# GateLoop attention with a SwiGLU feed-forward on one core: norm roots spread through a line in device memory, ten pairs by 15 products, group 0 in chunks, and a schedule with other costs and dates

## The chip, the cores and the metric

The kernel runs on one core of one Trainium2 chip. The metric is the device time of one execution in microseconds (us), with all data in device memory at the start and the output there at the end. Smaller is better. Five engines work side by side: TensorE (PE, the matrix products; PEld is its weight load), VectorE (DVE), ScalarE (ACT), GpSimd (POOL) and SyncE (SP, which here only issues transfers). Each runs its own instructions strictly in the order in which they were written, so one instruction that waits holds up all behind it on that engine.

## The reference

Two blocks follow one another. The first is a gated linear attention with complex decay (batch 4, 8 heads, 768 steps, head size 48); the second is an RMS norm with a SwiGLU feed-forward (3072 tokens, width 384, hidden width 1536).

```python
mag = np.sqrt(a_re * a_re + a_im * a_im)
scale = np.minimum(mag, 0.999) / (mag + 1e-06)
a_re_n, a_im_n = (a_re * scale, a_im * scale)
for t in range(S):
    new_re = ar * S_re - ai * S_im
    new_im = ar * S_im + ai * S_re
    S_re, S_im = (new_re + kv, new_im)          # kv: outer product of k and v at t
    y[:, :, t] = np.einsum('bhd,bhde->bhe', q[:, :, t], S_re)
...
xn = x / np.sqrt(np.mean(x * x, axis=-1, keepdims=True) + 1e-06) * rms_g
g = xn @ w_gate
return (g * (1.0 / (1.0 + np.exp(-g))) * (xn @ w_val)) @ w_out
```

## The kernel before

**Chunks, units and groups.** The 3072 tokens are 24 chunks (n = 0 to 23) of 128. The decays of the first two chunks are worked out one by one (units 0 and 1), then two chunks at a time (units 2 to 12). The feed-forward takes two chunks together, a group: group g holds chunks 2g and 2g + 1.

**A unit (`gates`).** ACT takes squares, roots, arctangent and sines, and DVE takes running products and running sums over time. This gives the turned queries and keys. In a buffer called `rot` (and, for later chunks, in place in `kin`) they stand in the order of the input; six DMAs of SP per chunk put them into `kq`, where the heads lie as the products want them. For units 0 and 1 the decay at the end of the chunk is spread by DVE into `ot` and by a small PE product `bank<-ot,ot`; for later units by small DMAs (`decay<-ends`).

**A chunk (`attend`).** PE makes the scores (`bank<-kq`, 32 rows at a time); DVE masks them into `am` (`COPY_PREDICATED`); PE makes the output y from `am`, `ve` (the values), `kq` and `state`, and the new state (`bank<-ident,kq`, ACT copies to `kt`, then `bank<-vn,kt`). For the norm, ACT squares y into `sq`, PE adds over features (`bank<-ones,sq`), DVE scales into `ssv`, and POOL takes the inverse root `rs`, one number per token, in a column over 128 partitions. It is wanted as a row on all partitions. For chunks 0 to 3, 22 and 23 PE does that (`bank<-ident,rs`). For chunks 4 to 21 (`SENT`) POOL sends two DMAs: `rs` into a line within partition 0 of `sq`, and that line to all partitions of `row`. Then DVE multiplies y by it into `xT`, the normalized input of the feed-forward.

**The feed-forward.** Groups 0 to 2 (`PLAIN = 3`) go through `feed`: per block b of six, three 128x256 products for each of two halves of `w_gate` and as many for `w_val`, ACT's Silu into `sg`, DVE's product into `hT`. Groups 3 to 11 go through `joint`: the product of the two chunks with the weights is made from 15 products with sums of weights and sums of inputs in place of 18. `forms` makes those sums of weights once, 28 operations of DVE on 128x512, into room that single chunks used before: `gin[1]`, `rots[1]`, `kqs[1]`, `ams[1]`. From chunk `SOLO = 6` on, therefore, only one buffer each of `kq`, `am` and `rot` is in use. Per group, 12 DVE operations on 128x128 make the sums of inputs. Products per block are 15, each four 128x128 matmuls. From group 2 on the second half of the feed-forward (`down`) also saves products. A 128x512 product with zeros (`bank<-zeros`) opens a bank where a sum must be added to.

**Weights.** `narrow` brings the float64 weights in pieces: POOL issues the DMA, ACT converts the low word, and three operations of DVE put the number together (`TENSOR_SCALAR`, `SCALAR_TENSOR_TENSOR`, and a third that the profile calls `CUSTOM_DVE_ANT_0` and the order listing `ISA`). Six pieces are for `wg` and `wv` (128x1536 each), six for `wo` (128x768 each). A one-element copy on POOL (`junk`) waits for each piece's landing.

**What sets the order.** All operations are collected in a list with their engine, an estimated duration and what they depend on. `Flow.dates` gives each a due time, back from the feed-forward products; a table `flow.shift` then moves single stages by some us. `Flow.schedule` plays the program through: each engine that is free takes, of its operations that are ready by the estimate, the one with the earliest due time. The estimates of that play (how long a DMA takes to land, what a change of engine costs) thus decide the order in which the instructions are written, and the chip then runs them in that order whatever the true times are. Where PE has nothing to do in the first 62 us, warm matmuls (`bank<-rot`) are put in.

```python
    SYNC = 0.12
    LAND = 2.0
...
                    o["landed"] = now + o["slow"] + self.LAND + (1.5 if o["eng"] == "POOL" else 0.0)
...
    PLAIN = 3
    WIDE = 12
    SOLO = 6
...
            line = sq[0:1, 1]
            dma(line, rss[n % 2], "POOL", slow=SLOW)
            dma(wide, line.unsqueeze(1).to_broadcast([1, P, C]), "POOL", slow=SLOW)
```

Nearly all instructions carry the line of `Flow.issue` (L715) in the profile, so they are told apart by the names of what they write and read.

Of the kernel before, what the change touches and what calls it, by code (L numbers as in the profile page):

```python
# [8 lines left out]
FP32 = mybir.dt.float32  # L9
# [9 lines left out]
P = 128  # L19
# [481 lines left out]
class Flow:  # L501
# [6 lines left out]
    SYNC = 0.12  # L508
    LAND = 2.0
# [4 lines left out]
    TABLES = {"silu": ("S",), "sin": ("S", "T"), "arctan": ("T",), "rsqrt": ("A",)}  # L514

    def __init__(self, nc, rooms):
        self.nc = nc
        self.rooms = rooms
        self.ops = []
        self.seen = {}  # L520
        self.stage = None
        self.shift = {}
        self.warm = None
        self.fillers = []

# [36 lines left out]
    def add(self, eng, calls, dur, reads=(), writes=(), table=None, land=None, due=None, after=(), behind=(), late=None, mode=None, group=None):  # L562
        op = dict(i=len(self.ops), eng=eng, calls=calls, dur=dur, deps=set(), table=table, land=land,
# [31 lines left out]
    def schedule(self):  # L595
# [6 lines left out]
        mode = None  # L602
# [5 lines left out]
        lanes = {}  # L608
        sent = []
        recent = []  # L610
        now = 0.0
        order = 0

        def release(o, end, users=users):
            for u in users[o["i"]]:
                x = self.ops[u]
                lat = self.SYNC if x["eng"] != o["eng"] or o["land"] is not None else 0.0
                ready[u] = max(ready[u], end + lat)
# [3 lines left out]

        def flows(t):
            busy = [q for q in lanes.values() if q]
            whole = sum(q[0][1]["packet"] for q in busy)
            for q in busy:
                q[0][0] -= (t - now) * q[0][1]["packet"] / whole

        while True:
# [10 lines left out]
            busy = [q for q in lanes.values() if q]  # L640
            if busy:
                whole = sum(q[0][1]["packet"] for q in busy)
                q = min(busy, key=lambda q: q[0][0] / q[0][1]["packet"])
                t = now + max(0.0, q[0][0]) * whole / q[0][1]["packet"]
                if best is None or t <= best[0]:
                    flows(t)
                    now = max(now, t)
                    o = q.pop(0)[1]
                    o["landed"] = now + o["slow"] + self.LAND + (1.5 if o["eng"] == "POOL" else 0.0)
# [31 lines left out]
            if eng == "PE" and o["mode"] != mode:  # L681
                mode = o["mode"]
                dur += 0.06
            if eng == "PE" and self.warm and t < self.warm["until"] and all("end" in x for x in self.warm["after"]):
                since = max([free["PE"]] + [x["end"] + self.SYNC for x in self.warm["after"] if not recent])
# [12 lines left out]
            free[eng] = t + dur  # L698
            release(o, t + dur, self.next)
            if o["land"] is not None:  # L700
                flows(t)
                now = max(now, t)
                if eng != "POOL":
                    sent.append(o)
                lanes.setdefault(eng, []).append([o["load"] + 0.05, o])
# [12 lines left out]
def fast(tc, ctx, qT, kT, v, a_re, a_im, w_gate, w_val, w_out, rms_g, out, H, bad):  # L718
# [19 lines left out]
    PLAIN = 3  # L738
    WIDE = 12
    SOLO = 6  # L740
# [16 lines left out]

    outside = {x.tensor.name for x in (qT, kT, v, a_re, a_im, w_gate, w_val, w_out, rms_g, out)}
    keep = []
    banks = []  # L760
# [38 lines left out]
    def scan(o, d0, d1, init, op0, op1, **kw):  # L799
        return add("DVE", [(nc.vector.tensor_tensor_scan, (),  # L800
                            dict(out=o, data0=d0, data1=d1, initial=init, op0=op0, op1=op1))],
                   0.10 + 2.38e-3 * cols(o), aps(d0, d1, init), [o], **kw)
# [12 lines left out]
    def act(o, x, func, scale=None, bias=None, accum=None, **kw):  # L815
# [5 lines left out]
        if accum is not None:  # L821
            k["accum_out"] = accum
        dur = 0.17 + 0.86e-3 * cols(o) + 0.09 * len(aps(scale, bias)) + (0.19 if accum is not None else 0.0)
        return add("ACT", [(nc.scalar.activation, (), dict(out=o, in_=x, func=func, **k))], dur,
                   aps(x, scale, bias), aps(o, accum), table=TABLE.get(func), **kw)
# [11 lines left out]
    def dma(o, x, eng="SP", slow=0.0, **kw):  # L837
# [4 lines left out]
        load = n / row * (0.006 + 50.3e-6 * row) / 16  # L842
        op = add(eng, [(QUEUE[eng].dma_start, (), dict(out=o, in_=x))], 0.85 if eng == "POOL" else 0.62, [x], [o],
# [3 lines left out]
        op["packet"] = max(0.07, 0.006 + 50.3e-6 * row * (2 if eng == "POOL" and row == 2048 else 1))  # L847
# [126 lines left out]
    def fetch(i, piece, raw, eng):  # L974
# [13 lines left out]
        if eng == "POOL":  # L988
            landed[i] = add("POOL", [(nc.gpsimd.tensor_copy, (), dict(out=junk, in_=raw[0:1, 1:2]))], 0.8,
                            after=[sent])  # L990
# [5 lines left out]
    def narrow(i):  # L996
# [3 lines left out]
        if ap.dtype == FP32:  # L1000
            dma(to, ap.rearrange("(c p) f -> p c f", p=P)[:, c, f:f + n], "POOL")
            return
# [672 lines left out]
```

## Time and profile before

| | us |
|---|---|
| three runs, median | 700.45 |
| three runs, lowest to highest | 699.45 to 700.63 |
| the profiled execution, its own time | 701.28 |
| its span, first to last instruction | 699.5 |
| granted TensorE clock over it | 0.989 of full |

The profile gives, for each engine, its busy time, the same in 40 slices of the span, the chain of work that ended last, and groups of instructions. The trace behind it lists single instructions: start in us from the span's start, duration in us, engine, line, operation, what it writes and reads, its shape, how many were put together, and in square brackets the idle time of the engine before it and what ended that. A matrix product in float32 counts as two matmuls in the trace and as one in the program.

### The profile page before, as it was taken

Reading aid. Unit: us, or ns where it says so; the run is one execution under the profiler, and the core shown is the slowest. Engines: PE = TensorE matmul, PEld = TensorE weight load, DVE = VectorE, ACT = ScalarE, POOL = GpSimd, SP = SyncE. Lnnn points to the kernel's source line nnn. Section 1 sums busy time; section 2 is a strip of 40 time slices with the busy share of each in tenths; the row PEclk is TensorE's granted clock in tenths of the full one; section 3 lists DMA queues with packets and bytes.
Section 4 is the critical chain, followed back from the end, with each engine's and each line's share of the span. In section 5 each row is a group of like instructions: output and inputs, shape, how many; then the busy total and the mean of one; then the engine's idle time right before and its main releaser. Section 6 shows DMA issues by size and latency. Waiting matters only on the chain.

```text
span 699.5 us, 18714 instructions
## 1 busy us (share of the span) xinstructions
PE 657.1 (94%) x7792; PEld 607.5 (87%) x7792; DVE 559.4 (80%) x1017; ACT 477.9 (68%) x807; POOL 59.7 (9%) x108
## 2 busy tenths in 40 slices
PE   0698999999999999999999999999999998999995
PEld 0587867886889999998999999999999998999995
DVE  8989888869888788888788889888898896356462
ACT  8657777898654675574675684675674884688884
POOL 3122100011000001000101010001000010000000
PEclk9989999999999999999999999999999999999999
DMA  9995462535424243434504334424623543834422
GB/s 292 291 290 178 154 166 75 148 65 106 111 57 103 60 82 62 134 77 86 128 17 80 96 70 96 126 60 86 133 53 75 119 97 112 250 94 145 149 72 91
DMA packets 104012, 81.98 MB, mean 117 GB/s; under 512 B 41936, under 2 KB 94416, under 8 KB 103920
## 3 DMA queue, kind: packets, MB, share of 16 engines
q1 hardware_dynamic: 98560, 64.78, 34.6%
q0 software_dynamic: 4416, 15.35, 10.3%
q8 instruction: 62, 1.02, 0.6%
q10 hardware_dynamic: 944, 0.59, 0.3%
q14 instruction: 30, 0.25, 0.1%
HBM read 55.84 MB, written 4.72 MB: 87 GB/s over the span
## 4 chain that ended last, share of the span: by engine, by line
PE 79%; DVE 7%; ACT 6%; DMA 3%; SPq 2%; issue 2%; POOL 0%; DVEq 0%; ACTq 0%
PE bank L715 79%; SPq L715 2%; DMA kq<-kin 2%; ACT turns L715 2%; ACT L715 1%; DVE hT L715 1%; DVE rot L715 1%; ACT t L715 1%; DVE wv L715 1%; DVE turns L715 1%; DMA in<-in_a_im_dram 1%; DVE wg L715 1%; DMA in<-in_a_re_dram 1%; DVE t L715 1%; DVE in L715 0%
## 5 line engine op out<-in xcount | busy, mean ns | idle before, releaser
L715 PE MATMUL bank<-wo,hT 128*128 128x192 f32 (+1 forms) x696 | 143.7, 352 | 0.9 <-DVE hT L715 0.9
L715 PEld LDWEIGHTS bank<-wo,hT 128*128 128x128 f32 x696 | 115.5, 191 | 13.3 <-DVE hT L715 1.8
L715 PE MATMUL bank<-xT,wg 128*128 128x128 f32 (+1 forms) x504 | 98.2, 330 | 0.0
L715 PE MATMUL bank<-xT,wv 128*128 128x128 f32 (+1 forms) x504 | 94.3, 321 | 0.0
L715 PEld LDWEIGHTS bank<-xT,wg 128*128 128x128 f32 x504 | 80.2, 194 | 7.4 <-issue 0.4
L715 PEld LDWEIGHTS bank<-xT,wv 128*128 128x128 f32 x504 | 79.1, 192 | 5.9 <-ACT turns L715 0.2
L715 ACT ACT_TABLE_LOAD x51 | 65.4, 1283 | 7.3 <-DVE t L715 2.8
L715 ACT ACTIVATE hT<-bank 128x512 f32<-128x512 f32 x90 | 52.4, 594 | 25.9 <-PE bank L715 23.1
L715 POOL TENSOR_TENSOR rs<-ssv,mhalf 128x1 f32<-128x1 f32 x24 | 20.6, 858 | 479.0 <-DVE ssv L715 428.3
L715 ACT ACTIVATE sg<-bank 128x512 f32<-128x512 f32 (+1 forms) x72 | 38.9, 540 | 21.1 <-PE bank L715 17.9
L715 DVE TENSOR_TENSOR hT<-hT 128x768 f32<-128x768 f32 (+1 forms) x58 | 50.5, 871 | 1.1
L715 ACT ACTIVATE bank<-bank 128x512 f32<-128x512 f32 x54 | 31.5, 583 | 26.8 <-PE bank L715 18.9
L715 ACT ACTIVATE kt<-bank 128x384 f32<-128x384 f32 x40 | 19.5, 489 | 43.9 <-PE bank L715 34.8
L715 DVE COPY_PREDICATED am<-causal,bank 128x512 f32<-128x512 int32 x48 | 34.7, 731 | 16.0 <-PE bank L715 15.9
L715 PE MATMUL bank<-yg,wg 128*128 128x128 f32 x288 | 45.7, 281 | 0.0
L715 PE MATMUL bank<-sums,hT 128*128 128x192 f32 x240 | 44.7, 328 | 0.1
L715 PE MATMUL bank<-yg,wv 128*128 128x128 f32 x288 | 43.9, 275 | 0.0
L715 DVE TENSOR_TENSOR hT<-bank,hT 128x512 f32<-128x512 f32 x45 | 30.9, 688 | 14.8 <-ACT bank L715 7.8
L715 PEld LDWEIGHTS bank<-kq 96*32 96x32 f32 x1536 | 31.3, 112 | 12.6 <-issue 4.5
L715 PE MATMUL bank<-kq 96*32 96x128 f32 (+3 forms) x1536 | 37.0, 240 | 5.4 <-DMA kq<-kin 3.6
L715 ACT ACTIVATE turns<-in 128x768 f32<-128x768 f32 (+1 forms) x39 | 30.4, 791 | 13.8 <-DVE kin L715 12.7
L715 PEld LDWEIGHTS bank<-sums,hT 128*128 128x128 f32 x240 | 39.3, 190 | 0.5 <-DVE yg L715 0.2
(216 smaller groups left out, 1417.4 us busy)
## 6 DMA issues: line engine op xcount, KB each, us to landing
kq<-rot SPq DMA_DIRECT2D x90, 128.0 KB, 2.5
kq<-kin SPq DMA_DIRECT2D x54, 128.0 KB, 2.7
kin<-in_q_dram SPq DMA_DIRECT2D x24, 192.0 KB, 3.2
kin<-in_k_dram SPq DMA_DIRECT2D x24, 192.0 KB, 3.4
out_dram<-ot SPq DMA_DIRECT2D x23, 192.0 KB, 2.8
in<-in_a_re_dram SPq DMA_DIRECT2D x11, 384.0 KB, 4.3
in<-in_a_im_dram SPq DMA_DIRECT2D x11, 384.0 KB, 4.2
vn<-in_v_dram SPq DMA_DIRECT2D x20, 192.0 KB, 2.6
```

The costliest lines, as they stand in the source:

```text
L715: fn(*args, **kw)
```

## The change

Six things are changed.

1. **The play's estimates.** DMAs land `LAND = 0.8` us after they are served instead of 2.0 (3.5 on POOL's queue), are served one after another instead of side by side, and have a lead of 1.2 or 1.9 us. Handing over between engines costs 0.03 to 0.2 us by who and whom, instead of 0.12. DVE and ACT overlap successive instructions by 0.083 and 0.1 us. Several durations are other numbers, such as the inverse root on POOL (2.0 us for chunks 0 and 1, then 0.6, instead of 1.2).
2. **Dates.** The table `flow.shift` has other entries.
3. **`PLAIN = 2`.** Group 2 goes through `joint` too, so ten groups do. The sums of weights (`forms`) are wanted one group earlier.
4. **`SOLO = 4`.** Chunks 4 and 5 use the single buffers too.
5. **The norm's row.** For chunks 4 to 21 the column of roots is written to a line in device memory, one of two in turn, and the line is read from there to all partitions.
6. **Group 0.** Its first three blocks (`SPLIT = 3`) are made for each chunk by itself, with 128 columns.

```diff
-    SYNC = 0.12
-    LAND = 2.0
+    LANDED = 0.11
+    OVERLAP = {"DVE": 0.083, "ACT": 0.1}
+    LAND = 0.8
...
-    TABLES = {"silu": ("S",), "sin": ("S", "T"), "arctan": ("T",), "rsqrt": ("A",)}
+    TABLES = {"silu": ("S",), "sin": ("S", "N"), "arctan": ("T",), "rsqrt": ("A",)}
...
+    def delay(self, o, x):
+        if o["land"] is not None:
+            return self.LANDED
+        if o["eng"] == x["eng"]:
+            return 0.034 if x["eng"] in self.OVERLAP else 0.0
+        if o["eng"] == "PE":
+            return 0.2
+        return 0.055 if x["eng"] == "PE" else 0.085 if x["eng"] == "POOL" else 0.034
...
-                    o["landed"] = now + o["slow"] + self.LAND + (1.5 if o["eng"] == "POOL" else 0.0)
+                    served = t + o["load"] + 0.05
+                    o["landed"] = served + o["slow"] + self.LAND
...
-    PLAIN = 3
+    PLAIN = 2
     WIDE = 12
-    SOLO = 6
+    SOLO = 4
...
+    dram = ctx.enter_context(tc.tile_pool(name="lines", bufs=1, space=DRAM))
+    lines_ = [dram.tile([1, C], FP32, name=f"line{i}", tag=f"line{i}") for i in range(2)]
...
-                                                        op=ALU.pow))], 1.2, [sv, mhalf], [rss[n % 2]])
+                                                        op=ALU.pow))], 2.0 if n < 2 else 0.6, [sv, mhalf], [rss[n % 2]])
         if n in SENT:
-            line = sq[0:1, 1]
-            dma(line, rss[n % 2], "POOL", slow=SLOW)
+            line = lines_[n % 2]
+            dma(line.rearrange("a t -> t a"), rss[n % 2], "POOL", lead=1.2)
             wide = row
-            dma(wide, line.unsqueeze(1).to_broadcast([1, P, C]), "POOL", slow=SLOW)
+            dma(wide, line.to_broadcast([P, C]), "POOL", lead=1.2)
...
+                if g == 0 and b < SPLIT:
+                    for t in range(2):
+                        flow.stage = "head", 2 * b + t
+                        list_ = []
+                        for i in range(2):
+                            f = b * 2 + i
+                            for d in range(ND):
+                                list_.append((o[:, i * T + t * C:i * T + (t + 1) * C],
+                                              w_[:, f // 4, d, f % 4 * P:(f % 4 + 1) * P],
+                                              xT[:, d, t * C:(t + 1) * C], d == 0, d == ND - 1))
+                        dur = 2 * ND * mm_time(C)
+                        clock[0] += dur * SPREAD
+                        mms(list_, dur, due=clock[0] - (1 - t) * dur)
...
-        ("attend", 8): 0.6, ("attend", 9): 3.8, ("attend", 11): 3.3, ("attend", 14): 1.6, ("attend", 15): -6.6,
+        ("attend", 3): -2.0, ("attend", 14): -2.4, ("attend", 15): -0.5, ("attend", 16): 23.5,
```

The order in which instructions are written moves nearly everywhere. Three places matter below.

The first is the start of TensorE's program, up to the scores of chunk 0. `ot` are the small products for the decays of units 0 and 1, `rot` the warm matmuls, `kq` the scores. Before:

```order
L715 MATMUL bank_65<-ot_134,ot_133 96x8 x3
L715 MATMUL bank_68<-rot_105 128x128 x38
L715 MATMUL bank_66<-ot_134,ot_133 96x8 x3
L715 MATMUL bank_68<-rot_105 128x128 x2
L715 MATMUL bank_69<-kq_107 32x128
```

Now:

```order
L722 MATMUL bank_69<-ot_138,ot_137 96x8 x3
L722 MATMUL bank_70<-ot_138,ot_137 96x8 x3
L722 MATMUL bank_72<-rot_109 128x128 x27
L722 MATMUL bank_73<-kq_111 32x128
L722 MATMUL bank_73<-kq_111 32x96
```

The product for unit 1 stood between the warm matmuls and the scores; it stands ahead of the warm matmuls now, and there are 27 of those.

The second place is VectorE's program from the turning of the first keys and queries to the masks `am` of chunk 0. `wv` and `wg` are the weights that are put together. Before:

```order
L715 TENSOR_TENSOR rot_106<-kin,turns 128x768 x2
L715 ISA wv<-wo,wv 128x3072
L715 TENSOR_SCALAR wg<-wo 128x1536
L715 SCALAR_TENSOR_TENSOR wg<-wo,wg 128x1536
L715 ISA wg<-wo,wg 128x3072
L715 TENSOR_TENSOR ends<-t_103,t_102 128x3
L715 TENSOR_TENSOR ot_134<-ends,ot_134 128x24
L715 TENSOR_SCALAR wv<-hT 128x1536
L715 COPY decay_110<-bank_66 96x8
L715 SCALAR_TENSOR_TENSOR wv<-hT,wv 128x1536
L715 COPY_PREDICATED am_115<-causal,bank_69 128x512
L715 COPY_PREDICATED am_115<-causal,bank_70 128x512
```

Now (`ends` and `ot` of unit 1 are rows further up, ahead of all weights):

```order
L722 TENSOR_SCALAR wv<-wo 128x1536
L722 COPY decay_114<-bank_70 96x8
L722 SCALAR_TENSOR_TENSOR wv<-wo,wv 128x1536
L722 TENSOR_TENSOR turns<-turns,t_106 128x2x384
L722 TENSOR_TENSOR rot_109<-kin,turns 128x768
L722 SCALAR_TENSOR_TENSOR in_102<-turns 128x384
L722 TENSOR_TENSOR rot_109<-kin,turns 128x768
L722 TENSOR_SCALAR wg<-wo 128x1536
L722 TENSOR_TENSOR turns<-turns,t_106 128x2x384
L722 TENSOR_TENSOR rot_110<-kin,turns 128x768 x2
L722 TENSOR_SCALAR wv<-hT 128x1536
L722 SCALAR_TENSOR_TENSOR wg<-wo,wg 128x1536
```

After this last row come one more weight operation and the two `am` rows. The small product for unit 1 no longer stands behind a whole piece of weights, and the third operation of both first pieces has moved behind the masks.

The third place is VectorE's program between the norm of chunk 5 (`ssv`) and its normalized input (`xT`), the last one that group 2 waits for. On 128x512, `in_99`, `rot_106`, `wg`, and in the changed kernel `wg`, `wv`, `rot_110`, `am_120`, are sums of weights; the other rows are work for later units. Before, from the row of `ssv` on:

```order
L715 TENSOR_SCALAR ssv<-bank_72 128x1
L715 TENSOR_TENSOR rot_105<-kin,turns 128x768
L715 TENSOR_TENSOR kin<-kin,turns 128x768
L715 TENSOR_TENSOR t_101<-t_101,t_102 128x768
L715 SCALAR_TENSOR_TENSOR in_99<-wg 128x512
L715 TENSOR_TENSOR in_99<-wg,in_99 128x512
L715 TENSOR_TENSOR rot_106<-wg,in_99 128x512
L715 SCALAR_TENSOR_TENSOR in_99<-wg,in_99 128x512
L715 TENSOR_TENSOR rot_106<-wg,in_99 128x512
L715 TENSOR_TENSOR turns<-in_98,turns 128x1536
L715 TENSOR_SCALAR t_101<-t_101 128x768
L715 SCALAR_TENSOR_TENSOR t_103<-t_102,t_101 128x128 x6
```

Now, whole:

```order
L722 TENSOR_SCALAR ssv<-bank_76 128x1
L722 TENSOR_TENSOR wg<-wg,rot_110 128x512
L722 TENSOR_TENSOR wv<-wv,am_120 128x512
L722 TENSOR_TENSOR rot_110<-wg,rot_110 128x512
L722 TENSOR_TENSOR am_120<-wv,kq_112 128x512
L722 TENSOR_TENSOR wg<-wg 128x512
L722 TENSOR_TENSOR wv<-wv 128x512
L722 TENSOR_TENSOR rot_110<-rot_110,wg 128x512
L722 TENSOR_TENSOR am_120<-am_120,wv 128x512
L722 TENSOR_TENSOR wg<-rot_110,wg 128x512
L722 TENSOR_TENSOR wv<-kq_112,wv 128x512
L722 TENSOR_TENSOR xT_101<-bank_75,row 128x3x128
```

Ten of the 28 sums of weights now stand between the two rows, ten stand ahead of `ssv`, and eight follow `xT`, the last of them 18 rows on. Before, one more row (`in_98<-turns`) stood ahead of `xT`, five sums had been written by then, and group 2 needed none of them.

More of the change, by code (lines that the diff above doesn't have):

```diff
@@ L680, in schedule @@
                 self.loads = getattr(self, "loads", 0) + 1
-            if eng == "PE" and o["mode"] != mode:
-                mode = o["mode"]
-                dur += 0.06
+            if eng == "PE":
+                dur += self.between(o, last)
+                mode, last = o["mode"], o
             if eng == "PE" and self.warm and t < self.warm["until"] and all("end" in x for x in self.warm["after"]):
-                since = max([free["PE"]] + [x["end"] + self.SYNC for x in self.warm["after"] if not recent])
+                since = max([free["PE"]] + [x["end"] + 0.06 for x in self.warm["after"] if not recent])
                 n = int((t - since - 0.3) / 0.43)
@@ L822, in act @@
             k["accum_out"] = accum
[L823 to L825 removed]
+        near = x.tensor.name in rooms and rooms[x.tensor.name][0].startswith("bank")
+        dur = (0.165 if near else 0.2) + 0.843e-3 * cols(o) + 0.09 * len(aps(scale, bias))
+        if x.dtype == U32:
+            dur += 0.09e-3 * cols(o)
+        op = add("ACT", [(nc.scalar.activation, (), dict(out=o, in_=x, func=func, **k))], dur,
+                 aps(x, scale, bias), aps(o, accum), table=TABLE.get(func), **kw)
+        if accum is not None:
+            op["over"] = 0.0
+        return op
     QUEUE = {"SP": nc.sync, "ACT": nc.scalar, "POOL": nc.gpsimd}
@@ L846, in dma @@
         op["load"] = load
-        op["packet"] = max(0.07, 0.006 + 50.3e-6 * row * (2 if eng == "POOL" and row == 2048 else 1))
+        op["lead"] = lead or (1.9 if eng == "POOL" else 1.2)
         return op
@@ L988, in fetch @@
         if eng == "POOL":
-            landed[i] = add("POOL", [(nc.gpsimd.tensor_copy, (), dict(out=junk, in_=raw[0:1, 1:2]))], 0.8,
+            landed[i] = add("POOL", [(nc.gpsimd.tensor_copy, (), dict(out=junk, in_=raw[0:1, 1:2]))], 0.25,
                             after=[sent])
@@ L1084, in send_decays @@
         ns = UNITS[u]
+        flow.stage = "decay", u
         if u < 2:
```

89 lines of the change are left out of this document (48 added, 41 removed), and 3 rows, old and new, of the table filler.

## The prediction

> **What bounds the kernel now.** I read the page first: which engine is full, where it isn't, and what the chain that ended last runs through.
>
> ```profile
> PE 657.1 (94%) x7792; PEld 607.5 (87%) x7792; DVE 559.4 (80%) x1017; ACT 477.9 (68%) x807; POOL 59.7 (9%) x108
> ...
> PE   0698999999999999999999999999999998999995
> ...
> PE 79%; DVE 7%; ACT 6%; DMA 3%; SPq 2%; issue 2%; POOL 0%; DVEq 0%; ACTq 0%
> ```
>
> PE is full except in the first slices and the last, and 79% of the chain is PE. So the time is PE's work plus the stretches in which it has none. The second view is the busy time by stretches, cut at the first product of group 0 (55.88), the first of group 2 (176.48) and near the end (columns: us, then PE, PEld, DVE, ACT, POOL busy, clock, DMA).
>
> ```profile
> 0.00:55.88 55.88, 28.40 (x416) 26.17 (x416) 49.94 (x80) 36.49 (x60) 15.90 (x39) 0.94 1.00 295
> 55.88:176.48 120.60, 119.02 (x1174) 94.14 (x1174) 101.38 (x150) 97.39 (x133) 12.19 (x19) 0.99 0.47 119
> 176.48:690.00 513.52, 506.93 (x6192) 484.75 (x6188) 406.37 (x783) 343.14 (x615) 31.61 (x50) 1.00 0.40 99
> 690.00:699.50 9.50, 2.75 (x19) 2.42 (x17) 1.74 (x5) 0.83 (x2) 0.00 (x0) 0.90 0.15 49
> ```
>
> Three quantities follow. The start lasts 55.88 us. From there to 690 PE idles only 1.58 + 6.59 = 8.2 us. The tail costs 9.5 us. VectorE idles 120.60 - 101.38 = 19.2 us in the second stretch. The third view is PE's timeline over the start.
>
> ```profile
> 22.32 10.09 PE L715 MATMUL bank<-rot 128*128 128x128 f32 x76 [4.24 <-DVE rot L715]
> 35.47 1.13 PE L715 MATMUL bank<-ot,ot 128*96 128x8 f32 x6 [3.06 <-DVE ot L715]
> 37.59 2.36 PE L715 MATMUL bank<-kq 96*32 96x128 f32 x64
> ...
> 55.88 4.52 PE L715 MATMUL bank<-xT,wg 128*128 128x256 f32 x12
> 60.24 2.75 PE L715 MATMUL bank<-xT,wv 128*128 128x256 f32 x12
> 62.83 2.75 PE L715 MATMUL bank<-xT,wg 128*128 128x256 f32 x12
> ```
>
> PE stood at the small product for unit 1 until 35.47 with the scores of chunk 0 behind it. Were those ready? The next rows answer, from VectorE, SP's queue and the DMA groups.
>
> ```profile
> 20.32 0.96 DVE L715 TENSOR_TENSOR turns<-turns,t 128x768 f32<-128x768 f32 x1 [1.14 <-ACT turns L715]
> 21.31 1.83 DVE L715 TENSOR_TENSOR rot<-kin,turns 128x768 f32<-128x768 f32 x2
> 23.05 0.55 DVE L715 SCALAR_TENSOR_TENSOR in<-turns 128x384 f32<-128x384 int32 x1
> 23.52 0.95 DVE L715 TENSOR_SCALAR wv<-wo 128x1536 int32<-128x1536 int32 x1
> 24.51 1.76 DVE L715 SCALAR_TENSOR_TENSOR wv<-wo,wv 128x1536 int32<-128x1536 int32 x1
> 26.19 0.95 DVE L715 TENSOR_TENSOR turns<-turns,t 128x768 f32<-128x768 f32 x1
> ...
> 35.24 0.18 DVE L715 TENSOR_TENSOR ot<-ends,ot 128x24 f32<-128x24 f32 x1
> ...
> 38.97 0.73 DVE L715 COPY_PREDICATED am<-causal,bank 128x512 f32<-128x512 int32 x1 [0.50 <-PE bank L715]
> ...
> 55.27 0.55 DVE L715 TENSOR_TENSOR xT<-yg,bank 128x384 f32<-128x384 f32 x1
> ```
>
> ```profile
> 22.30 3.86 SPq L715 DMA_DIRECT2D kq<-rot  x6
> ```
>
> ```profile
> kq<-rot SPq DMA_DIRECT2D x90, 128.0 KB, 2.5
> ```
>
> SP had issued the six transfers by 26.16, and one lands in 2.5, so `kq` of chunk 0 was there at about 28.7, some nine us before PE read it. What held PE was VectorE's order.
>
> **The start, step by step.** Now both small products precede the warm matmuls. VectorE does the first two weight operations (23.52 to 26.19, 2.67 us), one `in` (0.47) and unit 1's two small decay rows (0.3 for both, an estimate from the 0.18 of one) before the second `rot` ends; the wait of 1.14 ahead of `turns` covers some. So the pair, which ended at 23.14, ends at 23.14 + 2.67 + 0.47 + 0.3 - 1.14 = 25.4, and its first half, without the `in` and the second `rot`, at 24.0. Three more issues of 3.86 / 6 = 0.64 and 2.5 of landing put `kq` at 29.8. The 27 warm matmuls are 54 in the trace, at 10.09 / 76 = 0.133, so 7.2 us: they end at 31.2, and the scores begin there, 6.4 earlier than 37.59. `am` follows 1.38 later (38.97 - 37.59) at 32.6, but VectorE has six rows ahead of it after 25.4: two `TENSOR_SCALAR` of 0.99 (23.52 to 24.51), two `SCALAR_TENSOR_TENSOR` of 1.68 (24.51 to 26.19), `turns` of 0.99 (20.32 to 21.31) and the `rot` pair of 1.74 (21.31 to 23.05), 8.1 in all. That makes 33.5, which is 5.5 earlier.
>
> From `am` to the end of chunk 1's `xT` took 55.82 - 38.97 = 16.9. The 19 rows of VectorE that now lead from the one to the other add up to 15.7 without waits, by the durations that their kinds have in the trace, and I give the waits the 1.2 between. The chunkwise start of group 0 adds little: its first products are written behind chunk 1's `ident,rs`, so they skip only the writing of that chunk's `xT`, about 0.6 (55.88 - 55.27). So group 0 begins at 55.88 - 5.5 - 0.6 = 49.8: **-6.1**. Its ends: -3, when POOL's copy that waits for a weight piece (ahead of chunk 1's root in POOL's order now) is late and VectorE waits once more for a piece; -8, when the waits vanish and the `am` begins with the scores.
>
> **The products.** Group 2's first half was twelve sets of twelve 128x256 matmuls (24 per block over six blocks), at 62.83 - 60.24 = 2.59 a set: 31.1.
>
> ```profile
> 231.37 0.38 PE L715 MATMUL bank<-zeros 128*128 128x512 bf16 x1
> 231.59 0.50 PE L715 MATMUL bank<-ident,kq 96*128 96x96 f32 x4
> ...
> 246.11 0.61 PE L715 MATMUL bank<-yg,wg 128*128 128x128 f32 x4
> ...
> 249.24 0.61 PE L715 MATMUL bank<-xT,am 128*128 128x128 f32 x4
> ```
>
> Now it is 2 blocks x 15 products of eight matmuls. The second of the rows for it is seven sets of four behind the first with nothing between, 3.13 / 7 = 0.447 a set: 60 x 0.447 = 26.8. One more `zeros` is 0.22 (231.37 to 231.59). Group 0's six sets in chunks are 24 matmuls each at 0.1117, 2.68 for 2.59: +0.54. Sum -4.3 + 0.2 + 0.5 = **-3.5**, all on PE, in stretches that PE bounds.
>
> **VectorE ahead of group 2.** The sums of weights are wanted a group earlier, and the sums of inputs are new there.
>
> ```profile
> 167.43 0.69 DVE L715 TENSOR_TENSOR rot<-wg,in 128x512 f32<-128x512 f32 x1
> 168.04 0.69 DVE L715 SCALAR_TENSOR_TENSOR in<-wg,in 128x512 f32<-128x512 f32 x1
> ...
> 234.48 0.29 DVE L715 TENSOR_TENSOR ve<-yg,yg 128x128 f32<-128x128 f32 x1
> 234.69 0.28 DVE L715 TENSOR_TENSOR ve<-xT 128x128 f32<-128x128 f32 x1
> ```
>
> 28 x 0.61 = 17.1, of which five stood ahead of group 2 before, so 14.0 move; 12 x 0.21 = 2.5 are added. That is 16.5 of the 19.2 idle. But the rows of a later unit that stood between chunk 5's `ssv` and its `xT` have gone behind, so some more stays free. VectorE's rows from the first `am` to the last sum of weights now add up to 126, again by kind. Beginning at 33.5 it is through at 159.5 without waits, and with the idle share of before (19.2 / 120.6 = 0.16) at 33.5 + 126 / 0.84 = 183.5. PE comes to the products that need the last sums eight products of 0.9 behind the first, near 49.8 + 120.6 + 7.2 = 177.6. So the bounds are 0 and +6. I take 0: 18 us of waits fit in, and the order has something ready to do at most places where VectorE waited for one thing before. That chunks 4 and 5 use single buffers hangs on the same slack.
>
> **The other waits of PE,** 8.2 us before: all dates are new. Bounds -8 (gone) and +8 (twice as many); nothing in the trace picks one, so 0.
>
> **The roots through device memory.** 18 chunks take this way.
>
> ```profile
> 140.86 0.15 DVE L715 TENSOR_SCALAR ssv<-bank 128x1 f32<-128x1 f32 x1
> 153.58 0.55 DVE L715 TENSOR_TENSOR xT<-bank,row 128x384 f32<-128x384 f32 x1
> ```
>
> ```profile
> 144.25 0.55 POOL L715 DMA_DIRECT2D row<-sq  x1 [1.67 <-DMA sq<-rs]
> ```
>
> ```profile
> out_dram<-ot SPq DMA_DIRECT2D x23, 192.0 KB, 2.8
> ...
> ve<-in_v_dram SPq DMA_DIRECT2D x24, 96.0 KB, 3.0
> ...
> row<-sq POOLq DMA_DIRECT2D x18, 64.0 KB, 4.0
> ...
> sq<-rs POOLq DMA_DIRECT2D x18, 0.5 KB, 2.2
> ```
>
> The pair took 2.2 + 4.0 = 6.2. A write to device memory is between 2.2 and 2.8 by these rows, a read to all partitions between 3.0 and 4.0: 5.2 to 6.8, and I take 5.2, as 96 KB from device memory is nearest to the 64 KB of a row. For chunk 4 the row landed at 144.25 + 4.0 = 148.3 and `xT` came at 153.58, so 5.3 us of other work hid it. Cost **0**. That cover shrinks: for chunk 5 only ten sums of weights (6.1 us) stand between `ssv` and `xT` now, against 5.2 and the root itself before it. A row a little late costs VectorE's slack, not PE. The Trainium skill, page "DMA: Bandwidth & Descriptors", section "Anatomy of one DMA — SWDGE (gpsimd) path", speaks against the line: a DMA reports only once its last byte is confirmed in the target memory, and device memory is the heaviest target. By that the write alone would be the longer of the two ways; the 2.8 of the output rows beside the 2.2 leaves 0.6 for it here, and the sum would still not change while the cover holds.
>
> **The sum.** The profiled execution took 701.28, span and what lies around it: 701.28 - 6.1 - 3.5 = 691.7. The median of the three runs, 700.45, is 0.83 lower, so 690.9.
>
> **The rivals.**
> - *VectorE late at group 2* (+6): 696.9. For it: the share of idle time in that stretch; against it: the last sums aren't needed by the first eight products. 0.17.
> - *PE's waits vanish* (-8): 682.9. For it: most waits are of DMAs and hand-overs that the estimates now follow more closely; against it: no order has none. 0.10.
> - *The start doesn't come through*: the pieces of weights bind it rather than the order, DMA being full (share 1.00) until 55.88. Then only the products are left: 697.0. Against it: ACT had the fourth piece of `wg` and `wv` at 28.10 (the row below), long before PE came to it. 0.05.
>
> ```profile
> 28.10 1.68 ACT L715 ACTIVATE hT<-hT 128x1536 int32<-128x1536 uint32 x1 [1.28 <-DMA hT<-in_w_gate_dram]
> ```
>
> - *Slower: the row of roots comes late in every joint group.* The place is `xT` of each group's second chunk, which gates the sums of inputs and PE's second product. Each us beyond the cover costs ten groups 1 us. The estimate for a landing on POOL's queue fell from 2.0 + 1.5 + 2.0 to 0.8 after the service, so `xT` is written closer behind. It outweighs the gain of 9.6 from 1 us of lateness on; at 2 us it gives 690.9 + 20 = 711. For it: 4-byte writes of one column and a read of the same bytes are nowhere in this trace. Against it: 5.2 is under 6.2. 0.08. The rule of the Trainium skill named above would push this way.
>
> **How the numbers follow.** The forecast, both gains with waits as before within some 3 us, has 0.60 and its own range 687 to 695. The range 683 to 698.5 takes in the late VectorE, the start that fails and most of the vanishing waits, and leaves out the slower case. A measurement of this kernel can tell about 0.2%, 1.4 us. Faster by more: 0.60 + 0.10 + 0.05 + 0.12 of the late case's 0.17 (its upper end is within) = 0.87; within: 0.05; slower: 0.08.
>
> **What would show it.** In the changed profile PE's scores of chunk 0 should begin near 31 and group 0 near 49.8; if the small product for unit 1 still waits, the first step is wrong. Between group 0's start and group 2's `zeros` PE should idle 2 to 4 us; a wait for `wg`, `wv` or `xT` there is the first rival. Sixty 128x128 rows of four should take 26.8. Waits of PE for `xT` or `yg` at the head of the joint groups are the slower case. And the two DMAs of a line should take 5.2 to 6.8 together. A new wait of over 3 us that recurs per group would make the prediction wrong.

## The result, and the profile after

The changed kernel takes **857.01 us** (median of 4 runs, 853.07 to 865.95) where the kernel before took 700.02 beside it (699.45 to 700.63): a ratio of 1.2224, 95% interval 1.218 to 1.2267. It is 22% slower, and the forecast was 690.9. Ratios here and below, unlike the medians, leave out runs that are over 1.5% above the fastest of their kernel, such as the 865.95. The execution profiled took 853.07, its span 851.4.

The page of the changed kernel: busy time of each engine, PE and its granted clock in 40 slices, the chain that ended last.

```profile
PE 693.0 (81%) x7927; PEld 643.5 (76%) x7927; DVE 560.4 (66%) x1049; ACT 492.8 (58%) x839; POOL 81.0 (10%) x108
...
PE   1899899759779778799975978778779567989996
...
PEclk9999999979898898888997989799989798999999
...
DMA 31%; PE 26%; DVE 19%; ACT 13%; issue 6%; POOL 4%; SPq 0%; DVEq 0%; POOLq 0%; ACTq 0%
PE bank L722 26%; DMA line<-rs 15%; DMA row<-line 8%; POOL rs L722 3%; DVE hT L722 3%; DVE turns L722 3%; DVE t L722 2%; ACT rot L722 2%; ACT t L722 1%; ACT L722 1%; ACT kin L722 1%; DMA rot<-in_w_val_dram 1%; DVE rot L722 1%; DVE xT L722 1
```

PE was 79% of the chain and is 26% now; two transfers that had no share are 23%, and they are the two of the line. PE is full until the eighth slice, where the first chunk of the line comes, and falls to 5 to 7 tenths again and again behind. Cut as before (first product of group 0, head of group 2, near the end):

```profile
0.00:48.20 48.20, 24.44 (x430) 22.48 (x431) 44.58 (x77) 37.09 (x61) 14.04 (x36) 1.00 0.93 283
48.20:177.03 128.83, 119.79 (x1159) 95.36 (x1158) 102.74 (x153) 82.67 (x117) 24.89 (x21) 0.97 0.47 124
177.03:842.00 664.97, 545.69 (x6324) 522.81 (x6323) 411.99 (x818) 373.07 (x662) 42.04 (x51) 0.91 0.34 78
842.00:851.40 9.40, 3.11 (x20) 2.82 (x18) 1.11 (x2) 0.00 (x0) 0.00 (x0) 0.84 0.15 51
```

The start is 7.7 us shorter, and the tail as it was. The second stretch, where the first chunk of the line falls, is 8.2 us longer and takes the start's gain away again. Nearly all that is lost against the kernel before stands behind 177.03: PE idles 664.97 - 545.69 = 119.3 us there where it idled 6.6, and its clock is 0.91 where it was 1.00. The view of waits says at what (what waited, for what: us in all, times, longest), for VectorE, then POOL.

```profile
DVE xT L722 <- DMA row<-line: 133.4, 18, 12.9
...
POOL row L722 <- DMA line<-rs: 140.0, 18, 9.8
```

The DMA groups of the changed kernel (KB each, median us from issue to landing):

```profile
row<-line POOLq DMA_DIRECT2D x18, 64.0 KB, 4.3
decay<-ends SPq DMA_DIRECT2D x66, 1.0 KB, 3.2
...
line<-rs POOLq DMA_DIRECT2D x18, 0.5 KB, 8.0
```

The pair takes 8.0 + 4.3 = 12.3 us in place of 6.2, and VectorE, which works in order, stands at each of the 18 `xT`, 7.4 us in the mean. One of them, chunk 5, on the timelines of POOL, VectorE and PE:

```profile
167.62 6.36 POOL L722 TENSOR_TENSOR rs<-ssv,mhalf 128x1 f32<-128x1 f32 x1 [14.55 <-DVE ssv L722]
174.28 0.59 POOL L722 DMA_DIRECT2D line<-rs  x1 [0.29 <-POOL rs L722]
182.06 0.54 POOL L722 DMA_DIRECT2D row<-line  x1 [7.19 <-DMA line<-rs]
```

```profile
172.87 0.68 DVE L722 TENSOR_TENSOR wv<-kq,wv 128x512 f32<-128x512 f32 x1
186.45 0.56 DVE L722 TENSOR_TENSOR xT<-bank,row 128x384 f32<-128x384 f32 x1 [12.90 <-DMA row<-line]
```

```profile
177.69 0.61 PE L722 MATMUL bank<-xT,wv 128*128 128x128 f32 x4
187.07 1.22 PE L722 MATMUL bank<-xT,rot 128*128 128x128 f32 x4 [8.77 <-DVE xT L722]
188.08 1.06 PE L722 MATMUL bank<-xT,am 128*128 128x128 f32 x4
```

VectorE has done all that is written ahead of `xT` at 173.55 and idles 12.9; PE gets through two products and idles 8.77. The transfers are not alone in that: the root itself took 6.36 us here, where 0.56 is usual (the last section comes back to it). What comes behind such a gap is slower too: a set of four of the same shape takes 1.06 where it took 0.61. The granted clock from 187 to 190 is 0.50 of full.

### The profile page after: what moved, and what is told of

It is laid out like the page before. It is cut to its first block, busy times and chain, and to the rows that moved or that the text cites. A ratio compares the mean times of both kernels' runs of the same rounds, so it can differ in the third digit from the quotient of the medians.

```text
span 851.4 us, 19034 instructions
## 1 busy us (share of the span) xinstructions
PE 693.0 (81%) x7927; PEld 643.5 (76%) x7927; DVE 560.4 (66%) x1049; ACT 492.8 (58%) x839; POOL 81.0 (10%) x108
## 4 chain that ended last, share of the span: by engine, by line
DMA 31%; PE 26%; DVE 19%; ACT 13%; issue 6%; POOL 4%; SPq 0%; DVEq 0%; POOLq 0%; ACTq 0%
PE bank L722 26%; DMA line<-rs 15%; DMA row<-line 8%; POOL rs L722 3%; DVE hT L722 3%; DVE turns L722 3%; DVE t L722 2%; ACT rot L722 2%; ACT t L722 1%; ACT L722 1%; ACT kin L722 1%; DMA rot<-in_w_val_dram 1%; DVE rot L722 1%; DVE xT L722 1%; DMA in<-in_a_im_dram 1%
## 5 line engine op out<-in xcount | busy, mean ns | idle before, releaser
L722 PE MATMUL bank<-xT,wg 128*128 128x128 f32 (+1 forms) x500 | 89.1, 315 | 39.0 <-DVE ot L722 23.7
L722 DVE TENSOR_TENSOR xT<-bank,row 128x384 f32<-128x384 f32 x18 | 10.0, 558 | 133.4 <-DMA row<-line 133.4
L722 PE MATMUL bank<-xT,wv 128*128 128x128 f32 (+1 forms) x500 | 87.0, 310 | 0.1
L722 POOL TENSOR_TENSOR rs<-ssv,mhalf 128x1 f32<-128x1 f32 x24 | 34.1, 1422 | 480.3 <-DVE ssv L722 480.3
L722 PE MATMUL bank<-kq 96*32 96x32 f32 (+3 forms) x1536 | 40.5, 251 | 22.4 <-DVE am L722 9.3
L722 PE MATMUL bank<-yg,wg 128*128 128x128 f32 x320 | 53.3, 291 | 1.2 <-ACT hT L722 1.2
L722 PE MATMUL bank<-am,ve 128*32 128x128 f32 x768 | 41.3, 292 | 13.4 <-DVE xT L722 13.4
L722 PEld LDWEIGHTS bank<-yg,wg 128*128 128x128 f32 x320 | 44.3, 201 | 3.4 <-ACT hT L722 1.4
L722 ACT ACTIVATE sg<-bank 128x256 f32<-128x256 f32 (+1 forms) x72 | 38.4, 534 | 14.6 <-DVE hT L722 9.0
L722 PEld LDWEIGHTS bank<-yg,wv 128*128 128x128 f32 x320 | 44.0, 199 | 0.0
```

Of the source, the lines that this page charges most:

```text
L722: fn(*args, **kw)
```

## The experiments

Two theories for the loss. **Late row**: the line lands too late for the order, and VectorE stops in order. **Something else in the change**: its new order, prices, products and single buffers. And one question behind: why does a write of 512 bytes take 8.0 us?

**The line in SBUF again** (the on-chip buffers, where the kernel before had it). Every instruction stays where the changed planner, the play of `Flow.schedule`, put it; only where the two transfers go is edited.

```diff
-            dma(line.rearrange("a t -> t a"), rss[n % 2], "POOL", lead=1.2)
+            x = dma(line.rearrange("a t -> t a"), rss[n % 2], "POOL", lead=1.2)
+            x["calls"] = [(nc.gpsimd.dma_start, (), dict(out=near, in_=rss[n % 2]))]
...
```

> The changed kernel with every instruction in its place, but the line of roots lies in SBUF again (one line of 512 bytes in the first partition in place of the two in device memory). Theory, the line is late and VectorE stands at each xT in turn: the two transfers take 6.2 us in place of 12.3, so the 133.4 us of VectorE's waits for the row fall by some 18 x 6.1 = 110 to about 25, and the time to 700 to 735 us. Rival, the new order or its dates are bad in themselves (VectorE late with the sums, waits of PE elsewhere): the time stays above 800 us. If steps one to four of the prediction were right and the line's lateness is all gone: 691 us.

Measured: 740.82 us, 1.0557 times the kernel before (1.0494 to 1.0619). Its DMA groups, its waits of VectorE, and PE's timeline at the head of group 2:

```profile
kin<-in_q_dram SPq DMA_DIRECT2D x24, 192.0 KB, 2.8
...
row<-near POOLq DMA_DIRECT2D x18, 64.0 KB, 4.0
decay<-ends SPq DMA_DIRECT2D x66, 1.0 KB, 2.0
...
near<-rs POOLq DMA_DIRECT2D x18, 0.5 KB, 2.3
```

```profile
DVE xT L722 <- DMA row<-near: 46.7, 18, 6.9
```

```profile
170.40 0.38 PE L722 MATMUL bank<-zeros 128*128 128x512 bf16 x1
...
174.40 0.71 PE L722 MATMUL bank<-xT,rot 128*128 128x128 f32 x4 [2.73 <-DVE xT L722]
```

Where the line lies is worth 857.01 - 740.82 = 116 us. But 38 stay beside the 703.12 that the kernel before took with it, more than expected, since even the pair of 6.3 us is late by 46.7 / 18 = 2.6 a chunk in this order. The roots have a part in that: in this run too they took 6.36, 4.28, 4.21 and 3.56 at four chunks where the planner had 0.6. Over the 18 chunks they come to 19 us more than planned, so by estimate up to 19 of the 46.7 are theirs and not the transfers'. Until the second product of group 2 the forecast held: its head is at 170.40, 6.1 ahead of the kernel before.

**The kernel before, with the line in device memory,** again with no instruction moved.

```diff
             line = sq[0:1, 1]
-            dma(line, rss[n % 2], "POOL", slow=SLOW)
+            x = dma(line, rss[n % 2], "POOL", slow=SLOW)
+            x["calls"] = [(nc.gpsimd.dma_start, (), dict(out=far[n % 2].rearrange("a t -> t a"), in_=rss[n % 2]))]
...
```

> The kernel before with every instruction in its place, but the line of roots in device memory as in the change. In its trace xT comes 7.1 to 15 us, mostly 9.9, behind the issue of the row, and the row lands in 4.0, so the order holds some 5.9 us of cover; the line adds about 6.1. Theory, the price is the lateness beyond the cover: VectorE waits for a row 0 to 3 us a chunk, 15 to 20 us over 18 chunks, and PE feels part of it: 700 to 720 us. Rival, the line costs by itself wherever it stands (its small writes hold up the other transfers or POOL): over 780 us. If the write takes what the prediction said (5.2 to 6.8 for both transfers): 700 us, as before.

Measured: 745.77 us, 1.0593 times (1.051 to 1.0675). Its waits for transfers, from the longest of its runs (756.96, which the ratio leaves out), for PE and VectorE:

```profile
PE bank L715 <- DMA kq<-kin: 12.1, 3, 5.8
...
DVE kin L715 <- DMA ve<-in_v_dram: 10.0, 2, 7.8
...
DVE kin L715 <- DMA kin<-in_q_dram: 7.3, 2, 6.5
...
PE bank L715 <- DMA decay<-ends: 6.2, 3, 2.1
...
DVE xT L715 <- DMA row<-line: 2.4, 3, 1.7
```

Neither theory fits. The order does cover the row here, to 2.4 us in all, and the time is 43 us longer all the same. PE and VectorE wait instead for other transfers, which SP issues: PE's wait for `kq<-kin` was 3.8 in the kernel before and VectorE's for loads 1.8. So the line seems to do harm apart from being late, and my expectation of 700 to 720 missed that. The waits were read in the longest run alone, and these rows do not add up to the 43; the writes that nobody reads, below, test it.

**No line at all.** TensorE spreads the roots for all chunks, as it does for six of them anyway; the planner makes a new order of it.

```diff
-    SENT = range(4, N - 2)
+    SENT = ()
```

> The changed kernel with no line at all: TensorE spreads the roots of every chunk with one product, as it did for the first four and last two chunks, and ScalarE copies the chunk out of its bank for that; the planner sets the order anew with its own dates. It adds 18 products of 0.3 us and 18 copies of 0.55 us. Theory, the late line is the cause: 690 to 705 us, with no long wait of VectorE at xT. Rival, the other parts of the change (new prices and dates, products of fifteen for group 2, single buffers from chunk 4) bring the loss: over 780 us.

Measured: 727.09 us, 1.0349 times (1.0293 to 1.0405), between the two expectations. It tells little: its order is a new one, and the dates were fitted to another program. The run without row waits, below, is the one that separates the rest of the change.

**What kind of write is slow.** Two writes that nobody reads go behind each row of the kernel before, of seven kinds in turn.

```diff
+            for i in range(2):
+                kind = kinds[(2 * (n - 4) + i) % 7]
...
+                x = dma(o, s, "SP" if kind == "viasp" else "POOL", slow=SLOW, after=[x])
```

> The kernel before with two more transfers behind the row of each of the 18 chunks, whose results nobody reads, in turn of seven kinds: the column of roots as 128 pieces of 4 bytes into device memory, close together (dense), 64 bytes apart (spaced), 512 bytes apart (apart); one row of 512 bytes (whole); 128 pieces of 64 bytes (pieces); 128 pieces of 512 bytes (full), all on POOL's queue; and the close column on SP's queue (viasp). Time about 700 us, up to 710. Theory A, small pieces that fall close together in device memory wait for one another: dense and viasp about 8.0 us from issue to landing, spaced and apart 2.5 to 4, whole 2.5 to 3. Theory B, any 128 pieces of 4 bytes into device memory take so long: spaced and apart 8 as well. Theory C, any write into device memory from POOL's queue does: whole and full about 8 too, viasp about 3. The prediction had 2.2 to 2.8 for all.

Its DMA groups:

```profile
full<-row POOLq DMA_DIRECT2D x5, 64.0 KB, 2.6
sq<-rs POOLq DMA_DIRECT2D x18, 0.5 KB, 2.3
dense<-rs POOLq DMA_DIRECT2D x6, 0.5 KB, 8.9
spaced<-rs POOLq DMA_DIRECT2D x5, 0.5 KB, 4.1
apart<-rs POOLq DMA_DIRECT2D x5, 0.5 KB, 4.1
whole<-row POOLq DMA_DIRECT2D x5, 0.5 KB, 2.0
pieces<-row POOLq DMA_DIRECT2D x5, 8.0 KB, 1.7
```

Of the three theories A fits. Device memory is not slow to write: 64 KB of it take 2.6. The same 128 pieces of 4 bytes take 2.3 into SBUF, and into device memory 4.1 when they are 64 or 512 bytes apart and 8.9 when they lie side by side. The seven kinds do not all stand in the same place, though. Whole, pieces and full read the row, so they go out when it has landed; dense, spaced and apart go out about half a us or one us behind the row's issue, while it is under way with its own 3.9. So the 4.1 is no price of the distance: the runs below have a whole row of 512 bytes in that place, and it takes 3.9. The 8 to 9 of the close pieces is their own, as the changed kernel shows: its line has no such row ahead and takes 8.0. The write on SP's queue left no landing in the trace, so whether it depends on the queue stays open. The Trainium skill, page "DMA: Bandwidth & Descriptors", section "Specifications", says that pieces under 512 bytes are done by read-modify-write. Pieces side by side would then read and write the same stretch one behind the other; the 8.9 beside 4.1 agrees, though nothing here shows the reading itself, and 64-byte pieces at 1.7 show no such price. Why close pieces are slow stays open.

The time was 725.96 in its one run, against an expected 710 at most: writes that nobody waits for seem to cost time. That, with the kernel before and its line in device memory, gave the next three.

**Writes that nobody reads, one kind at a time,** behind each of the 18 rows of the kernel before, nothing else moved.

```diff
+            dma(extra.rearrange("a t -> t a"), rss[n % 2], "POOL", slow=SLOW, after=[x])
...
```

> The kernel before, its line in SBUF, with one more transfer behind each row: the column of roots as 128 pieces of 4 bytes close together into device memory, as the change writes it, read by nobody and waited for by nobody. Theory, such a write holds up other transfers that are under way (decays, kq, chunks of v), which PE then waits for: 715 to 745 us, as in the kernel before with the line in device memory, where VectorE waited only 2.4 us for rows in all. Rival, the 745 us there came from the row being late: 700 us, up to 703.

> As the run with extra close writes, but the 128 pieces of 4 bytes fall 64 bytes apart; they landed in 4.1 us where the close ones took 8.9. Theory, what holds up the others is the time that the pieces wait for one another: half of the loss or less, 700 to 715 us. Rival, the 128 small packets are what costs, wherever they fall: the same time as with the close writes.

> As the run with extra close writes, but 512 bytes of zeros from one partition, which landed in 2.0 us (as the 512 bytes of one row did): 698 to 702 us by each theory; if it is slower too, one more transfer on POOL's queue is what costs, and the extra runs say nothing of the kind of write.

Measured, against 702.05 of the kernel before: close 722.32 (ratio 1.0292, 1.019 to 1.0394); 64 bytes apart 700.54 (0.9998, 0.9969 to 1.0028); whole 702.19 (1.0023, 0.9991 to 1.0054). Only the close ones cost, some 20 us for 18 writes. The DMA groups of the three runs, one line each, compare the writes in the same place, half a us behind the row's issue:

```profile
dense<-rs POOLq DMA_DIRECT2D x18, 0.5 KB, 8.1
...
spaced<-rs POOLq DMA_DIRECT2D x18, 0.5 KB, 3.9
...
whole<-zeros POOLq DMA_DIRECT2D x18, 0.5 KB, 3.9
```

Spaced pieces land no later than one whole row of 512 bytes; both land just behind the row that went ahead of them. How the close ones cost, at one of them: POOL's timeline, the chain of waits, and VectorE's timeline of the run with close writes.

```profile
247.99 0.54 POOL L715 DMA_DIRECT2D dense<-rs  x1
```

```profile
249.25 10.81 DMA kin<-in_q_dram
```

```profile
260.19 0.96 DVE L715 TENSOR_TENSOR kin<-kin,t 128x768 f32<-128x768 f32 x1 [7.43 <-DMA kin<-in_q_dram]
```

SP issues the load of `kin` 1.3 us behind the close write, and VectorE is released by it 10.8 us after that issue. The trace has no landing of this write; the others of the run took 6.9 to 9.5, so if it was like them it was through by 257.5, and the load came 2.6 us or more behind it. In the kernel before SP issues the same load at the same place, a load of `kin` lands in 3.2 in the median, and VectorE works on it 7 us earlier, without a wait:

```profile
253.21 0.95 DVE L715 TENSOR_TENSOR kin<-kin,t 128x768 f32<-128x768 f32 x1
```

```profile
kin<-in_q_dram SPq DMA_DIRECT2D x24, 192.0 KB, 3.2
```

So a close write holds up what another queue sends meanwhile. The changed order shows it in the medians: with its line in SBUF, instruction for instruction the same, the loads of `kin` land in 2.8 and the decays in 2.0 (first run above), and with the line in device memory in 4.9 and 3.2:

```profile
kin<-in_q_dram SPq DMA_DIRECT2D x24, 192.0 KB, 4.9
```

The 20 us are half of the 43 that the kernel before lost with its line in device memory. There the row also comes over 5 us later (7.7 + 4.1 for the pair); what the other half is was not taken apart.

**No wait for a row.** The changed kernel without the 36 transfers; the row holds ones, so 18 chunks are not divided by their roots.

```diff
+            x["calls"] = []
...
```

> The changed kernel with every instruction of the engines in its place, without the 36 transfers of the line: the row is set to ones once at the start, so the 18 chunks are not divided by their root, which is left out. VectorE then waits for no row. Theory, the row is the whole loss and the rest of the prediction held: 691 us, 687 to 697. Rival, part of the loss over 700 us comes from the order or the prices of the change: 705 us or more, with waits of TensorE that have nothing to do with a row.

Measured: 697.68 us, 0.9932 times the kernel before (0.9895 to 0.9969), some 4.8 us less. Its page and PE by stretches:

```profile
PE 649.8 (93%) x7925; PEld 607.9 (87%) x7927; DVE 559.9 (80%) x1049; ACT 492.2 (70%) x839; POOL 59.5 (9%) x73
```

```profile
170.00:690.00 520.00, 509.17 (x6342) 490.78 (x6343) 410.83 (x818) 372.38 (x662) 23.11 (x19) 1.00 0.36 98
```

Without the line nothing of the loss is left: all of it comes from the way of the row, by its lateness or by what it holds up. The rest of the change gains, but half of what was forecast.

**A version with the row priced.** The line in SBUF, the planner told what it takes there, and the dates fitted anew by a search over the planner's own order.

```diff
-                                                        op=ALU.pow))], 2.0 if n < 2 else 0.6, [sv, mhalf], [rss[n % 2]])
+                                                        op=ALU.pow))], 2.0 if n < 2 else 0.9, [sv, mhalf], [rss[n % 2]])
...
-            dma(line.rearrange("a t -> t a"), rss[n % 2], "POOL", lead=1.2)
+            x = dma(line.rearrange("a t -> t a"), rss[n % 2], "POOL", lead=1.2, slow=0.3)
...
-            dma(wide, line.to_broadcast([P, C]), "POOL", lead=1.2)
+            x = dma(wide, line.to_broadcast([P, C]), "POOL", lead=1.2, slow=1.8)
...
```

> The changed kernel with the line in SBUF and the planner told what the runs showed for it (write 2.3 us, row 4.0, root 0.9), and with new dates fitted by search to these prices, so every order is new. Theory, lateness was what remained of the loss once the line was back in SBUF (46.7 us of VectorE's waits at xT, 741 us): the waits at xT fall to under 10 us in all and the time to that of the order without row waits, 697.7, or a little over: 696 to 706 us. Rival, the waits at xT go but VectorE then comes late elsewhere, since 6.3 us of cover have to be found for 18 chunks: over 710 us.

Measured: 697.83 us, 0.9937 times the kernel before (0.9917 to 0.9958). Its wait for rows:

```profile
DVE xT L722 <- DMA row<-near: 3.5, 4, 2.2
```

This is faster than both kernels, by a small 0.6% than the one before, with an interval clear of 1. It has the start and the products of the change, and the row is hardly ever late. Prices and dates were changed together, so the run does not tell what each is worth.

**The row from SP's queue** (the edit is against the version before).

```diff
-            x["calls"] = [(nc.gpsimd.dma_start, (), dict(out=wide, in_=near.unsqueeze(1).to_broadcast([1, P, C])))]
+            x["calls"] = [(nc.sync.dma_start, (), dict(out=wide, in_=near.unsqueeze(1).to_broadcast([1, P, C])))]
...
```

> As the run with the row priced, but both transfers of the line are issued by SP instead of POOL, with dates of their own. The decays, 1 KB from SBUF to SBUF on SP's queue, land in 2.0 us and the 128 KB of kq in 2.5 to 2.7, against 2.3 and 4.0 on POOL's. Theory, the pair then takes about 4.6 us in place of 6.3 and needs less cover: 1 to 3 us under the run with the row priced. Rival, SP's queue holds the row behind other transfers and their landings (it issues in order), so the row is no earlier: the same time or up to 10 us more.

Measured: 725.77 us, 1.0363 times (1.0318 to 1.0407). Its DMA groups and wait:

```profile
row<-near SPq DMA_DIRECT2D x18, 64.0 KB, 4.1
...
near<-rs SPq DMA_DIRECT2D x18, 0.5 KB, 2.0
```

```profile
DVE xT L722 <- DMA row<-near: 18.0, 10, 6.2
```

The row takes 4.1 from SP as it takes 4.0 from POOL, so its length isn't the queue's; planned for 2.9 (1.2 of lead, 0.3 of service, 0.6 and 0.8), it is late again. The 18.0 do not explain all of the 28 us over the version before it, which neither expectation had. Its dates are its own as well; the rest was not taken apart.

## Why the prediction was wrong, step by step

- **The start** (-6.1, group 0 at 49.8): right in its mechanism; it came to -7.7 here and to -4.6 in the run without row waits. PE's timeline of the changed kernel has the scores a little later than forecast (31.2) and group 0 a little earlier:

```profile
32.43 1.33 PE L722 MATMUL bank<-kq 96*32 96x128 f32 x64
...
48.20 5.52 PE L722 MATMUL bank<-xT,wg 128*128 128x128 f32 x48
```

- **The products** (-3.5) were not measured alone. A set of four takes 0.45 where none of them waits, as forecast (177.24 to 177.69 in the changed kernel).
- **VectorE ahead of group 2** (0, up to +6): the 0 held nearly. With the line in SBUF group 0 begins 7.2 us earlier, at 48.63, and the head of group 2 still 6.1. Between the two VectorE waits 1.07 for chunk 4's row.
- **The other waits of PE** (0, -8 to +8): without row waits PE idles 520.00 - 509.17 = 10.8 between 170 and 690, a few us more than the 6.6 in the nearly equal stretch before. That, and a start that varies (its group 0 began at 51.27), is where -4.8 falls short of the forecast's -9.5.
- **The roots through device memory** (0): this step failed, in its transfer time and in its cover. First the time: "A write to device memory is between 2.2 and 2.8 by these rows". The 2.8 was of output rows, 192 KB in long pieces; it bounds nothing for 4-byte pieces side by side, which took 8.0. The prediction had named that such writes "are nowhere in this trace", and still took the lower end. Second the cover: 5.3 us were read at chunk 4 of an order that planned over 11 us for the pair (2.0 + 1.5 + 2.0 behind the service of each transfer), and carried into one that planned some 4.4 (1.2 of lead, the service and 0.8 for each). What the planner doesn't plan it doesn't leave. By 46.7 us of waits, even the 6.2 of before would have been late in the new order, so the sum would have failed with the right transfer time as well. The root's own time, which the prediction names at chunk 5 and gives no size, belongs here too: 6.36 there.
- **The slower rival** named the place, but not its size. It counted one late row in each of ten groups, 1 us per us. All 18 chunks wait: from the run with no row to the line in SBUF, 46.7 us of VectorE's waits cost 740.82 - 697.68 = 43.1, so 0.92 per us. If that rate holds, the 86.7 us more of waits in the changed kernel make 80 of the 116 between it and the line in SBUF; the other 36 are an estimate of what the close writes do to the other transfers, and were not measured by themselves in that order.

PE shows the loss in two parts. Against the run with no row it idles (851.4 - 693.0) - (698.5 - 649.8) = 109.7 us more, and is busy 43.2 us longer with the same work, at a granted clock of 0.92 for 0.991. By the clock alone the 649.8 would become 649.8 x 0.991 / 0.92 = 700, an estimate, so the lower clock is enough to explain the 693.0. Part of each long wait that empties PE is paid again in the matmuls behind it.

The chance of 0.08 for the slower side rested on "5.2 is under 6.2", an estimate set against a measurement, though the same list says that such writes are in no row. The rule of the Trainium skill that the prediction cites (page "DMA: Bandwidth & Descriptors", section "Anatomy of one DMA — SWDGE (gpsimd) path") pointed the right way, but by luck: the 0.6 us that I left for it were 5.8, and not for its reason. A whole row of 512 bytes landed in device memory in 2.0 and 64 KB in 2.6, against 2.3 for the column into SBUF. What cost was that the pieces lie side by side, of which that rule says nothing.

## What to carry to other kernels

A transfer's time is taken from a row of the same kind: the same target, the same size of piece, the same distance between pieces; where there is none, the range has no known end (6.8, the far end here, was too short as well), and such a transfer is measured first. And when a change lowers a planner's price for a transfer, the old cover is gone with the old price: ask first what the new order leaves between the issue and its reader. An engine that works in order turns each late row into its own stop, for every chunk.

## What the chip showed unexpectedly

Writes of 4 bytes side by side into device memory not only take 8 to 9 us for 128, against 2.3 into SBUF and at most the 3.9 of a whole row in the same place when they are spaced; 18 of them cost a kernel that never waits for them some 20 us. At one of them a load issued beside it came after 10.8 us, where 3.2 is the median without such writes.

POOL's root, one column, takes 0.56 us at its best among the 18 chunks, and 6.36 at chunk 5, while VectorE runs sums of two SBUF tensors without a gap until 173.55 (the root ends at 173.98). In the changed kernel 4 of the 18 took over 3.5 us, and in the run with the line in SBUF, in the same order, the same four. The Trainium skill, page "GPSIMD Engine Reference", section "1. Specifications", says that GpSimd shares its SBUF interfaces with VectorE, whose instructions with two SBUF inputs contend with it; the rows agree, and suggest that a run of such instructions can keep a short one of POOL waiting to its end; no run here took them away to test it.
